# Retention attention and a top-2 mixture of experts on one core: a PSUM bank for VectorE's scratch, y in two parts, x's low part behind the routing steps

## The chip, the cores and the metric

The kernel runs on one core of a Trainium2 chip. A core has five engines that work side by side: PE (TensorE, matmuls into PSUM), DVE (VectorE), ACT (ScalarE), POOL (GpSimd) and SP (it issues DMAs). The metric is the device time of one execution in microseconds (us); less is better.

## What is computed

The reference has two parts. A retention attention runs over 4 batches of 768 tokens with 8 heads of 64; its output x, 3072 tokens of 512 numbers, goes to a mixture of 8 experts, of which each token takes the two with the highest noisy logits.

```
gamma = 1.0 - 2.0 ** (-5.0 - np.arange(H))
for t in range(S):
    state = gamma * state + einsum('bhd,bhe->bhde', k[:, :, t], v[:, :, t])
    y[:, :, t] = scale * einsum('bhd,bhde->bhe', q[:, :, t], state)
...
noisy_logits = x @ w_gate + log1p(exp(x @ w_noise)) * noise
top2 = argpartition(-noisy_logits, 2, axis=1)[:, :2]
top2_w = softmax of the two logits
for e in range(E):
    for k in range(2):
        mask = top2[:, k] == e
        h = np.maximum(x[mask] @ w1[e], 0.0)
        out[mask] += top2_w[mask, k, None] * (h @ w2[e])
```

## The kernel before, in words

The order of the work on each engine is the order in which the code issues it; nothing moves an instruction afterwards.

**The chunk loop (L704 to L732)** runs over 24 chunks of 128 tokens, j = 0 to 23, six for each batch (c = j % 6). An iteration j holds pieces of several chunks. On PE stand in this order: `qk(j+1)` (L335, scores into PSUM tiles pA), `x_total(j-1)` (L371, one matmul that sums the squares of y(j-1) into a few columns called XSS), what the table `between` holds for j, `y_mm(j)` (L349: masked scores times v; L352: q times the state U, not in a batch's first chunk; L362: the state update into the tile pU, not in a batch's last chunk), `x_rows(j-2)` (L386), `logits(j-2)` (L399, L402, into the tile pL) and what the table `todo` holds for j. y goes to one of two PSUM tiles pY, so y(j) may be written only when all readers of y(j-2) are done.

From y two f16 numbers are made whose sum is x: `x_hi` (ACT, L376) and `x_lo` (DVE, L380), both after a power-of-two scale that DVE computes from XSS (L169, L170). DVE also masks the scores (`masked(j+1)`, L342). ACT copies the state from pU to U (L368), squares y (L357) and copies x's rows (L388).

**Routing** of a batch starts when its logits are there and is cut in steps that stand in `between` and `todo`, so that they run in the iterations of the next batch: route_a and route_b (noisy logits, the top 2, L412 to L438), route_b2 and route_c (one-hot masks, L445 to L469), route_d (places in the sorted lists, L491 to L511, it reads pL), route_e (two parts, L521 and L525, it prepares a table), table (PE, L532), route_f (DVE, L537 or L539, it copies the table's result out of pL) and route_w (gates, L477 to L484). In the last iterations of a batch's turn, route_d stands at j = 10, 16 and 22 behind `x_lo(j-1)`. DVE's scratch for these steps lies in PSUM, in the columns of pU behind the state, so in the tile that PE writes at L362 and ACT reads at L368.

**The weights** of the first two experts come in f32 and are cut in f16 high and low parts during the loop: w_sum and w_hi and part of w_scaled on ACT (L193, L214, L226), w_scaled and w_rest on POOL (L228, L232), their scale on PE and DVE (L196, L203).

**After the loop** `early(n)` issues n units of the first expert's matmuls (first its first matrix, L751 to L753, whose result ACT reads at L754 and DVE at L755; then its second, L790 to L792) between the routing steps of the last batch. `ranks()` (L552 to L577) orders the other seven experts by their number of tokens; it is cut in two halves with one unit behind each, then come route_w and three units more. The expert loop (L891 to L963) follows.

Of the kernel before, what the change touches and what calls it, by code (L numbers as in the profile page):

```python
# [10 lines left out]
F32 = mybir.dt.float32  # L11
# [83 lines left out]
def moe_kernel(ctx, tc, qT, kT, kt, vt, noise, wgn, w1, w2, ctab, qtab, xbuf, gbuf, out):  # L95
# [49 lines left out]
    PL = pL[:, 0:NC * 4 * E].rearrange("p (c s e) -> p c s e", c=NC, s=2)  # L145
    XSS = pR[:, 0:4]
    POS = pL[:, 200:200 + (NC + 1) * NL].rearrange("p (c e) -> p c e", c=NC + 1)
    LST = pL[:, 280:280 + NCOL]
    SUM = pL[:, 340:348]
    pU = psum.tile([128, 512], F32, name="pU")  # L150
    PU = pU[:, :HP * D].rearrange("p (a d) -> p a d", a=HP)

    def spare(o, n):
        return pU[:, HP * D + o:HP * D + o + n]

    lanes = spare(0, 64).bitcast(F16)
    blks = spare(64, NCOL // 2).bitcast(F16)
    lidx = spare(92, NL), spare(102, NL)
    cump = spare(112, NL)
    small = spare(124, 48)  # L160
    invp = [spare(172 + i * NC, NC) for i in range(2)]
    wide = spare(184, NC * NL).rearrange("p (c e) -> p c e", c=NC)

# [179 lines left out]

    def y_mm(j):
        c = j % NC
        pY = psum.tile([128, HP, C], F32, name="pY", bufs=2)
        for i in range(HP):
            for s in range(2):
                nc.tensor.matmul(pY[s * 64:s * 64 + 64, i, :], VP[j][:, 2 * i + s, :], AM[j][:, s, i, :],  # L349
                                 start=(i == 0), stop=True, skip_group_check=True)  # L350
        for i in range(HP if c else 0):
            nc.tensor.matmul(pY[:, i, :], U[c % 2][:, i, :], QS[j][:, i, :],  # L352
                             start=False, stop=True, skip_group_check=True)
        PY[j] = pY.rearrange("p a c -> p (a c)")
        SS[j] = work.tile([128, 1], BF, name="xss")
        with nc.allow_low_precision(reason="only the exponent of the sum is used"):
            nc.scalar.activation(junk[:, :DM], PY[j], AF.Square, accum_out=SS[j])  # L357
        if c < NC - 1:

            for i in range(HP):  # L360
                for s in range(2):
                    nc.tensor.matmul(PU[s * 64:s * 64 + 64, i, :], IN["kt", j][:, i * 128 + s * 64:i * 128 + s * 64 + 64],  # L362
                                     VP[j][:, 2 * i + s, :],
                                     start=(c == 0 and i == 0), stop=True, skip_group_check=True)
            un = U[(c + 1) % 2]
            for s in range(2):
                r = slice(s * 64, s * 64 + 64)
                nc.scalar.activation(un[r, :, r], PU[r], AF.Copy)  # L368

# [182 lines left out]
    def ranks():  # L552
# [15 lines left out]
        nc.vector.tensor_copy(eid, rk)  # L568
        yield
        tp = hp.tile(s4, F32, name="tp")  # L570
# [82 lines left out]

    between = {}
    for b in range(B - 1):
        n = (b + 1) * NC - 1
        steps = [(2, route_a, b), (3, route_b, b), (4, route_b2, b), (4, route_c, b), (5, route_d, b),
                 (6, route_e, b, 0), (7, route_e, b, 1), (8, table, b), (8, route_w, b)]
        if b == B - 2:
            steps = steps[:-3]  # L660
        else:
            between.setdefault(n + 9, []).append((route_f, b))
        between.setdefault(n + 5, []).append((places, b))
        if b == B0 - 1:

            between[n + 9] += [(rows_of, acc, 0, 3)]
            between.setdefault(n + 10, []).extend((gather, 0, t, 0, 128, B0 * S) for t in range(3))
            for t in range(3):
                at(n + 11, x_t, 0, t)
        for s in steps:  # L670
            at(n + s[0], *s[1:])
    at(0, gate_sum)
    at(1, gate_weights)
    for i in range(4):
# [5 lines left out]
        at(8 + i, w_load, 0, "2", i)  # L680
        at(12 + i, w_sum, 0, "2", i)
        at(17 + i, w_hi, 0, "2", i)
        at(18 + i, w_scaled, nc.scalar, 0, "2", i)
        between.setdefault((19, 20, 22, 23)[i], []).append((w_rest, 0, "2", i))
    for i in range(7):
# [7 lines left out]
    between.setdefault(10, []).append((w_scale, 0, "1"))  # L693
    between.setdefault(17, []).append((w_scale, 0, "2"))
    mid = SECOND // 128
# [8 lines left out]
    for j in range(NCH):  # L704
# [5 lines left out]
        if j + AHEAD < NCH:  # L710
            load(j + AHEAD, "qk")
        if j:
            x_total(j - 1)
            x_hi(j - 1)
        if j + 1 < NCH:
            masked(j + 1)
        if j:
            x_lo(j - 1)
        if j + AHEAD < NCH:
            load(j + AHEAD, ("v", "kt"))  # L720
        if j >= 3:
            x_store(j - 3)
        for f, *a in between.get(j, []):
            f(*a)
# [3 lines left out]
        if j >= 2:  # L728
            x_rows(j - 2)
            logits(j - 2)  # L730
        for f, a in todo.get(j, []):
            f(*a)  # L732
    x_store(NCH - 3)
# [104 lines left out]
    x_lo(NCH - 1)  # L838
    route_e(b - 1, 1)
    early(1)  # L840
    x_rows(NCH - 1)
# [7 lines left out]
    for t in range(3, mid + 1):  # L849
        x_t(0, t)  # L850
    early(1)
    route_a(b)
# [23 lines left out]
    early(1)  # L876
    for piece in ranks():
        early(1)
    route_w(b)
    early(3)  # L880
    out_scale(0, 3, mid)
# [185 lines left out]
```

## Time and profile before

| | us |
|---|---|
| median of 3 runs | 684.81 (684.1 to 686.17) |
| the profiled execution's own time | 685.8 |
| its span, from the first to the last instruction | 684.0 |
| PE busy within the span | 651.6 (95%) |
| ACT busy | 318.7 (47%) |
| POOL busy | 291.5 (43%) |
| DVE busy | 278.1 (41%) |
| mean granted clock of TensorE | 0.981 |

A line of the timeline has the start of a group of like instructions in us from the start of the span, the time from its first start to its last end, the engine, the line of the kernel, the operation with output and input, the number of instructions, and in brackets how long the engine stood idle ahead of it and what ended that. Matmuls overlap, so the time that a group takes from PE is best read from start to start. The granted clock is 1.00 when TensorE runs at 2.4 GHz and 0.50 at 1.2 GHz. In the expert loop PE is at work almost without a break; its idle time lies in the chunk loop, in the routing behind it and at the two ends.

### The profile page before, as it was taken

Reading aid. Unit: us, or ns where it says so; the run is one execution under the profiler, and the core shown is the slowest. Engines: PE = TensorE matmul, PEld = TensorE weight load, DVE = VectorE, ACT = ScalarE, POOL = GpSimd, SP = SyncE. Lnnn points to the kernel's source line nnn. Section 1 sums busy time; section 2 is a strip of 40 time slices with the busy share of each in tenths; the row PEclk is TensorE's granted clock in tenths of the full one; section 3 lists DMA queues with packets and bytes.
Section 4 is the critical chain, followed back from the end, with each engine's and each line's share of the span. In section 5 each row is a group of like instructions: output and inputs, shape, how many; then the busy total and the mean of one; then the engine's idle time right before and its main releaser. Section 6 shows DMA issues by size and latency. Waiting matters only on the chain. (4 is left out here: it accounts for less than half of the span.)

```text
span 684.0 us, 12921 instructions
## 1 busy us (share of the span) xinstructions
PE 651.6 (95%) x5165; PEld 395.5 (58%) x5165; DVE 278.1 (41%) x765; ACT 318.7 (47%) x564; POOL 291.5 (43%) x226
## 2 busy tenths in 40 slices
PE   8999898998999999999999999999999999999991
PEld 5888787655666545654555455545554565456440
DVE  4768696774135435342144214420532152225100
ACT  5698777621157425452544345433543454434110
POOL 4547797312432534533443345234524451443131
PEclk9999899999999999999999999999999999999996
DMA  9999896424798435753665467446644663661132
GB/s 342 357 406 406 305 394 233 127 65 86 283 165 201 149 68 126 181 187 60 127 162 191 74 110 200 156 77 120 182 157 92 124 172 140 111 125 14 17 46 33
DMA packets 95230, 112.36 MB, mean 164 GB/s; under 512 B 62208, under 2 KB 62464, under 8 KB 91584
## 3 DMA queue, kind: packets, MB, share of 16 engines
q1 hardware_dynamic: 81472, 84.03, 37.5%
q0 software_dynamic: 13120, 26.63, 21.6%
q8 instruction: 42, 0.69, 0.4%
q10 hardware_dynamic: 576, 0.84, 0.4%
q14 instruction: 20, 0.16, 0.1%
HBM read 72.03 MB, written 26.34 MB: 144 GB/s over the span
## 5 line engine op out<-in xcount | busy, mean ns | idle before, releaser
L781 POOL DMA_INDIRECT out<-ot,idx x54 | 88.0, 1630 | 263.0 <-ACT ot L776 139.4
L751 PE MATMUL pH<-xe,w1h 128*128 128x384 f16 (+4 forms) x544 | 176.3, 324 | 2.8 <-DVE hl L755 2.7
L752 PE MATMUL pH<-xe,w1h 128*128 128x384 f16 (+4 forms) x544 | 176.3, 324 | 1.7 <-issue 1.7
L753 PE MATMUL pH<-xe,w1l 128*128 128x384 f16 (+4 forms) x544 | 176.3, 324 | 0.0
L755 DVE SCALAR_TENSOR_TENSOR hl<-pH,hh 128x384 f16<-128x384 f32 (+4 forms) x136 | 74.4, 550 | 214.1 <-ACT hh L754 195.5
L792 PE MATMUL pO<-w2h,hl 128*128 128x512 f16 x384 | 145.5, 379 | 0.0
L791 PE MATMUL pO<-w2l,hh 128*128 128x512 f16 x384 | 145.5, 379 | 0.0
L790 PE MATMUL pO<-w2h,hh 128*128 128x512 f16 x384 | 145.5, 379 | 0.0
L754 ACT ACTIVATE hh<-pH 128x384 f16<-128x384 f32 (+4 forms) x136 | 65.6, 484 | 130.6 <-PE pH L753 120.8
L776 ACT ACTIVATE ot<-pO,gse 128x512 f32<-128x512 f32 (+4 forms) x54 | 37.1, 686 | 174.1 <-PE pO L792 163.5
L645 POOL DMA_INDIRECT gx<-gbuf,idx x54 | 68.2, 1264 | 37.2 <-DMA gbuf<-gateb 21.5
L219 DVE SCALAR_TENSOR_TENSOR w1l<-wst,wsc,w1h 128x1024 f16<-128x1024 f32 x28 | 35.7, 1284 | 99.0 <-ACT w1h L214 96.3
L752 PEld LDWEIGHTS <-w1h 128*128 128x128 f16 x544 | 53.5, 98 | 37.1 <-issue 4.3
L753 PEld LDWEIGHTS <-w1l 128*128 128x128 f16 x544 | 53.5, 98 | 35.1 <-issue 1.1
L751 PEld LDWEIGHTS <-w1h 128*128 128x128 f16 x544 | 54.1, 99 | 32.9 <-issue 0.2
L635 POOL DMA_INDIRECT xg<-xbuf,idx x55 | 53.7, 976 | 42.3 <-issue 15.5
L193 ACT ACTIVATE junk<-wst 128x1024 bf16<-128x1024 f32 x64 | 67.0, 1047 | 0.1
L792 PEld LDWEIGHTS <-hl 128*128 128x128 f16 x384 | 37.5, 98 | 45.4
L790 PEld LDWEIGHTS <-hh 128*128 128x128 f16 x384 | 38.1, 99 | 44.1
L791 PEld LDWEIGHTS <-hh 128*128 128x128 f16 x384 | 37.5, 98 | 44.0
L308 POOL TENSOR_TENSOR vp<-in_v,ct 128x512 f32<-128x512 f32 x24 | 25.1, 1044 | 33.3 <-issue 21.3
L214 ACT ACTIVATE w2h<-wst,wsc 128x1024 f16<-128x1024 f32 x32 | 36.5, 1139 | 0.0
(173 smaller groups left out, 750.6 us busy)
## 6 DMA issues: line engine op xcount, KB each, us to landing
wst<-w SPq DMA_DIRECT2D x28, 1024.0 KB
in_q<-qT SPq DMA_DIRECT2D x24, 256.0 KB
in_k<-kT SPq DMA_DIRECT2D x24, 256.0 KB
in_v<-vt SPq DMA_DIRECT2D x24, 256.0 KB
xbuf<-xr SPq DMA_DIRECT2D x24, 256.0 KB
out<-zero SPq DMA_DIRECT2D x6, 1024.0 KB
in_kt<-kt SPq DMA_DIRECT2D x20, 256.0 KB
wst<-w SPq DMA_DIRECT2D x8, 512.0 KB
```

The lines of the kernel that those rows point to most:

```text
L193: nc.scalar.activation(junk, st[:, i * 1024:(i + 1) * 1024], AF.Square, accum_out=ss[:, i:i + 1])
L635: nc.gpsimd.indirect_dma_start(out=x[:p1], out_offset=None, in_=xbuf[:128 + rows], in_offset=bass.IndirectOffsetOnAxis(ap=idx[:p1, i:i + 1 ...
L645: nc.gpsimd.indirect_dma_start(out=GX[e][:, t, :], out_offset=None, in_=gbuf[:128 + rows], in_offset=bass.IndirectOffsetOnAxis(ap=idx[:, i ...
L751: nc.tensor.matmul(p[:, :n], whi, xh, start=(k == 0), stop=False)
L752: nc.tensor.matmul(p[:, :n], whi, xl, start=False, stop=False)
L753: nc.tensor.matmul(p[:, :n], wlo, xh, start=False, stop=(k == KT - 1))
L754: nc.scalar.activation(hh[:, f, n0:n1], p[:, :n], AF.Relu)
L755: nc.vector.scalar_tensor_tensor(hl[:, f, n0:n1], p[:, :n], 0.0, hh[:, f, n0:n1], op0=OP.max, op1=OP.subtract)
L781: nc.gpsimd.indirect_dma_start(out=out, out_offset=bass.IndirectOffsetOnAxis(ap=idx[:n, i:i + 1], axis=0), in_=ot[:n], in_offset=None, com ...
L790: nc.tensor.matmul(p, a, WT["2h"][:, f, :], start=(f == 0), stop=False)
L791: nc.tensor.matmul(p, a, WT["2l"][:, f, :], start=False, stop=False)
L792: nc.tensor.matmul(p, c, WT["2h"][:, f, :], start=False, stop=(f == FT - 1))
```

## The change

1. **PSUM.** DVE's scratch moves from pU to pR, which is then used by nothing else. XSS moves from pR to pL, the tile of the logits and places. pU holds the state alone.
2. **y in two parts.** `y_in(j)` (the masked scores times v) is cut out of `y_mm(j)` and stands ahead of `x_total(j-1)`; `masked(j+1)` stands ahead of `x_hi(j-1)`. U's part stays behind `between`.
3. **x's low part.** `x_lo(j-1)` moves to the end of iteration j, behind everything that `between` and `todo` issue there. route_a moves behind it (table `late`).
4. **Weights.** For the first expert's second matrix w_sum comes two iterations later, w_hi too, its scale at 19 instead of 17; of w_scaled on ACT one piece stays in the loop and three move behind it, together with all four w_rest on POOL.
5. **ranks()** is issued in one piece, then route_w, then four units in a row.

```
-    XSS = pR[:, 0:4]
+    XSS = pL[:, 352:356]
-    lanes = spare(0, 64).bitcast(F16)
...
+    lanes = pR[:, 0:64].bitcast(F16)
...
-        steps = [(2, route_a, b), (3, route_b, b), (4, route_b2, b), (4, route_c, b), (5, route_d, b),
+        late.setdefault(n + 2, []).append((route_a, (b,)))
+        steps = [(3, route_b, b), (4, route_b2, b), (4, route_c, b), (5, route_d, b),
```
```
-        if j:
-            x_total(j - 1)
-            x_hi(j - 1)
         if j + 1 < NCH:
             masked(j + 1)
-        if j:
-            x_lo(j - 1)
...
+        y_in(j)
+        if j:
+            x_total(j - 1)
+            x_hi(j - 1)
         for f, *a in between.get(j, []):
             f(*a)
...
         for f, a in todo.get(j, []):
+            f(*a)
+        if j:
+            x_lo(j - 1)
+        for f, a in late.get(j, []):
             f(*a)
```
```
-        at(12 + i, w_sum, 0, "2", i)
-        at(17 + i, w_hi, 0, "2", i)
-        at(18 + i, w_scaled, nc.scalar, 0, "2", i)
-        between.setdefault((19, 20, 22, 23)[i], []).append((w_rest, 0, "2", i))
+        at(14 + i, w_sum, 0, "2", i)
+        at(19 + i, w_hi, 0, "2", i)
+    at(23, w_scaled, nc.scalar, 0, "2", 0)
...
     route_e(b - 1, 1)
+    for i in range(1, 4):
+        w_scaled(nc.scalar, 0, "2", i)
+        w_rest(0, "2", i - 1)
...
-    for piece in ranks():
-        early(1)
+    ranks()
     route_w(b)
-    early(3)
+    early(4)
```

Three places show it in the engines' own order. On PE, in an iteration without a state update, before (pA are the scores, pR holds XSS, pY is y):

```order
L335 MATMUL pA<-qs,in_k 128x128 x8
L371 LDWEIGHTS oneb
L371 MATMUL pR<-xss,oneb 128x1
L349 MATMUL pY<-am,vp 64x128 x8
L352 MATMUL pY<-qs,U_162 128x128 x4
```

and after:

```order
L331 MATMUL pA<-qs,in_k 128x128 x8
L344 MATMUL pY<-am,vp 64x128 x8
L369 LDWEIGHTS oneb
L369 MATMUL pL<-xss,oneb 128x1
L350 MATMUL pY<-qs,U_162 128x128 x4
```

y's first part has moved ahead of the sum of squares of the chunk before. On DVE in iteration 10, before, from the masking of the scores of chunk 11 to the start of route_d (L491); x_1011 is the x of chunk 9:

```order
L342 TENSOR_TENSOR am<-pA,ct 128x512 x2
L380 SCALAR_TENSOR_TENSOR x_1011<-pY,upx,x_1011 128x512
L203 TENSOR_REDUCE s_1029<-pL 128x1
L169 TENSOR_SCALAR p2m<-s_1029 128x1
L170 TENSOR_SCALAR wsc_489<-p2m 128x1
L173 TENSOR_SCALAR wsc_489<-p2m 128x1
L491 TENSOR_TENSOR pU<-pL,cb 128x60
L492 TENSOR_TENSOR sl<-pL,cb 128x60
```

and after, from route_d's first instruction (L489) to the masking for chunk 12; x_1027 is the x of chunk 9:

```order
L489 TENSOR_TENSOR pR<-pL,cb 128x60
L490 TENSOR_TENSOR sl<-pL,cb 128x60
L492 TENSOR_TENSOR ps<-pL,cb 128x60
L493 SCALAR_TENSOR_TENSOR pR<-pR,sl 128x60
L494 TENSOR_TENSOR pR<-pL,cb 128x10
L500 TENSOR_TENSOR t<-pR,oh 128x120
L504 TENSOR_REDUCE pR<-t 128x12
L505 CAST pR<-pR 128x12
L506 TENSOR_SCALAR pR<-pR 128x12
L507 TENSOR_SCALAR pR<-pR 128x12
L509 CAST lf<-pR 128x24
L378 SCALAR_TENSOR_TENSOR x_1027<-pY,upx,x_1027 128x512
```

x_lo (L380, now L378) has moved from ahead of route_d to behind its last instruction. On DVE at ranks(), before (hl is the low part of a unit's result):

```order
L567 TENSOR_REDUCE rk<-cm 128x7
L568 CAST eid<-rk 128x7
L755 SCALAR_TENSOR_TENSOR hl<-pH,hh 128x192
L572 TENSOR_TENSOR tp<-acc,pm 128x343
L573 TENSOR_REDUCE tk<-tp 128x49
L547 TENSOR_SCALAR padv<-tk,ct 128x49
```

and after, at the same place:

```order
L565 TENSOR_REDUCE rk<-cm 128x7
L566 CAST eid<-rk 128x7
L569 TENSOR_TENSOR tp<-acc,pm 128x343
L570 TENSOR_REDUCE tk<-tp 128x49
L545 TENSOR_SCALAR padv<-tk,ct 128x49
```

The unit's instruction has left the middle of ranks(); the four of its kind now stand in a row behind route_w's last instruction (L482).

## Rows read from the trace of the kernel before

**Rows 1.** The page: busy time, share of the span and instructions of each engine.

```profile
PE 651.6 (95%) x5165; PEld 395.5 (58%) x5165; DVE 278.1 (41%) x765; ACT 318.7 (47%) x564; POOL 291.5 (43%) x226
```

**Rows 2.** The timeline of PE in iteration 8, from one qk to the next, at full clock.

```profile
42.96 1.16 PE L335 MATMUL pA<-qs,in_k 64*128 64x128 f32 x16
...
44.16 1.09 PE L349 MATMUL pY<-am,vp 128*64 128x128 f32 x16
45.19 1.16 PE L352 MATMUL pY<-qs,U 128*128 128x128 f32 x8
46.27 0.69 PE L362 MATMUL pU<-vp,in_kt 128*64 128x64 f32 x16
46.89 0.62 PE L386 MATMUL pX<-id,x 128*128 128x128 f16 x8
...
47.63 0.38 PE L335 MATMUL pA<-qs,in_k 64*128 64x128 f32 x2
```

**Rows 3.** The timeline of PE from iteration 10 to the last y: the qk of iterations 10, 14, 15, 20 and 21, the stalls between, and y(23).

```profile
52.30 1.16 PE L335 MATMUL pA<-qs,in_k 64*128 64x128 f32 x16
...
77.55 0.18 PE L399 MATMUL pL<-wg,x 128*128 128x32 f16 x1 [2.35 <-DVE acc L537]
...
77.84 2.08 PE L335 MATMUL pA<-qs,in_k 64*128 64x128 f32 x16
...
85.36 0.38 PE L335 MATMUL pA<-qs,in_k 64*128 64x128 f32 x2
...
95.15 0.18 PE L399 MATMUL pL<-wg,x 128*128 128x32 f16 x1 [0.88 <-DVE s L203]
...
111.10 0.18 PE L399 MATMUL pL<-wg,x 128*128 128x32 f16 x1 [2.35 <-DVE acc L539]
...
111.37 1.99 PE L335 MATMUL pA<-qs,in_k 64*128 64x128 f32 x16
...
117.93 1.16 PE L335 MATMUL pA<-qs,in_k 64*128 64x128 f32 x16
...
120.04 0.19 PE L458 MATMUL pL<-mb,trib 128*128 128x60 bf16 x1 [0.84 <-DVE mb L448]
...
124.02 1.09 PE L349 MATMUL pY<-am,vp 128*64 128x128 f32 x16
```

**Rows 4.** Windows: the stretch, its length, busy time of PE, PEld, DVE, ACT and POOL with the number of instructions, granted clock, DMA share, GB/s.

```profile
78.00:84.00 6.00, 6.00 (x43) 5.21 (x45) 3.81 (x26) 2.59 (x4) 3.36 (x2) 0.50 1.04 396
94.00:97.00 3.00, 2.12 (x36) 1.84 (x35) 2.93 (x12) 2.66 (x4) 3.00 (x4) 1.00 1.05 398
112.00:114.00 2.00, 2.00 (x21) 1.76 (x19) 1.93 (x11) 2.00 (x3) 1.50 (x2) 0.50 0.38 136
170.00:172.00 2.00, 2.00 (x14) 1.84 (x13) 0.89 (x6) 0.00 (x0) 0.00 (x0) 0.50 0.26 24
```

**Rows 5.** The timelines of PE and of DVE at the end of iteration 10: the last logits, the next qk and x_total; route_d from its first instruction, the scale of the chunk behind it, and a x_lo. Then DVE's x_lo in iteration 14.

```profile
57.27 0.17 PE L402 MATMUL pL<-wg,x 128*128 128x16 f16 x1
57.37 1.16 PE L335 MATMUL pA<-qs,in_k 64*128 64x128 f32 x16
58.46 0.18 PE L371 MATMUL pR<-xss,oneb 128*128 128x1 bf16 x1
...
57.56 0.23 DVE L491 TENSOR_TENSOR pU<-pL,cb 128x60 f32<-128x60 f32 x1 [0.64 <-ACT U L368]
...
59.79 0.15 DVE L169 TENSOR_SCALAR p2m<-pR 128x1 int32<-128x1 int32 x1
...
61.24 0.74 DVE L380 SCALAR_TENSOR_TENSOR x<-pY,upx,x 128x512 f16<-128x512 f32 x1
...
76.62 0.75 DVE L380 SCALAR_TENSOR_TENSOR x<-pY,upx,x 128x512 f16<-128x512 f32 x1 [1.78 <-ACT x L376]
```

**Rows 6.** The timeline of DVE in iteration 11: route_e from its first instruction to the scale behind it.

```profile
61.90 0.50 DVE L521 TENSOR_TENSOR bb<-pU,lf 128x336 f16<-128x336 f16 x1
...
63.83 0.15 DVE L169 TENSOR_SCALAR p2m<-pR 128x1 int32<-128x1 int32 x1
...
64.08 1.28 DVE L342 TENSOR_TENSOR am<-pA,ct 128x512 f32<-128x512 f32 x2
```

**Rows 7.** The timelines of DVE and of PE at ranks(): the unit's instruction between its halves, the second half, route_w's first instruction, the next units; and PE's matmuls of these units, the first and the last of the 39 ahead of a stall, the stall, and the first start at full clock after 21 matmuls.

```profile
165.36 0.36 DVE L755 SCALAR_TENSOR_TENSOR hl<-pH,hh 128x192 f16<-128x192 f32 x1 [4.63 <-ACT hh L754]
165.64 0.76 DVE L572 TENSOR_TENSOR tp<-acc,pm 128x343 f32<-128x343 f32 x1
...
168.13 0.16 DVE L477 TENSOR_SCALAR pU<-den 128x6 f32<-128x6 f32 x1
...
169.49 0.88 DVE L755 SCALAR_TENSOR_TENSOR hl<-pH,hh 128x192 f16<-128x192 f32 x3
...
163.79 0.25 PE L751 MATMUL pH<-xe,w1h 128*128 128x192 f16 x1
...
166.93 0.25 PE L753 MATMUL pH<-xe,w1l 128*128 128x192 f16 x1
169.89 0.32 PE L751 MATMUL pH<-xe,w1h 128*128 128x192 f16 x1 [2.72 <-DVE hl L755]
...
173.08 0.25 PE L751 MATMUL pH<-xe,w1h 128*128 128x192 f16 x1
```

**Rows 8.** The timeline of PE: the longest stall behind that.

```profile
183.78 0.27 PE L752 MATMUL pH<-xe,w1h 128*128 128x256 f16 x1 [1.14 <-issue]
```

More of the change, by code (lines that the diff above doesn't have):

```diff
@@ L149, in moe_kernel @@
     SUM = pL[:, 340:348]
[L150 to L154, printed above, removed]
-    lanes = spare(0, 64).bitcast(F16)
[L157 to L162, printed above, removed]
+    XSS = pL[:, 352:356]
+    pU = psum.tile([128, HP, D], F32, name="pU")
+    lanes = pR[:, 0:64].bitcast(F16)
+    blks = pR[:, 64:64 + NCOL // 2].bitcast(F16)
+    lidx = pR[:, 92:92 + NL], pR[:, 102:102 + NL]
+    cump = pR[:, 112:112 + NL]
+    invp = [pR[:, 128 + i * 8:128 + i * 8 + NC] for i in range(2)]
+    wide = pR[:, 144:144 + NC * NL].rearrange("p (c e) -> p c e", c=NC)
+    small = pR[:, 208:208 + 48]
     def pow2(ss, target, up, down=None):
@@ L342, in masked, with y_in, y_mm @@
             nc.vector.tensor_tensor(AM[j][:, s], pA[s], mask[:, None, :].to_broadcast([128, HP, C]), op=OP.mult)
-    def y_mm(j):
-        c = j % NC
-        pY = psum.tile([128, HP, C], F32, name="pY", bufs=2)
+    def y_in(j):
+        PY[j] = psum.tile([128, HP, C], F32, name="pY", bufs=2)
         for i in range(HP):
             for s in range(2):
-                nc.tensor.matmul(pY[s * 64:s * 64 + 64, i, :], VP[j][:, 2 * i + s, :], AM[j][:, s, i, :],
+                nc.tensor.matmul(PY[j][s * 64:s * 64 + 64, i, :], VP[j][:, 2 * i + s, :], AM[j][:, s, i, :],
                                  start=(i == 0), stop=True, skip_group_check=True)
+    def y_mm(j):
+        c, pY = j % NC, PY[j]
         for i in range(HP if c else 0):
@@ L361, in y_mm @@
                 for s in range(2):
-                    nc.tensor.matmul(PU[s * 64:s * 64 + 64, i, :], IN["kt", j][:, i * 128 + s * 64:i * 128 + s * 64 + 64],
+                    nc.tensor.matmul(pU[s * 64:s * 64 + 64, i, :], IN["kt", j][:, i * 128 + s * 64:i * 128 + s * 64 + 64],
                                      VP[j][:, 2 * i + s, :],
@@ L367, in y_mm @@
                 r = slice(s * 64, s * 64 + 64)
-                nc.scalar.activation(un[r, :, r], PU[r], AF.Copy)
+                nc.scalar.activation(un[r, :, r], pU[r], AF.Copy)
     def x_total(j):
@@ L568, in ranks @@
         nc.vector.tensor_copy(eid, rk)
-        yield
         tp = hp.tile(s4, F32, name="tp")
@@ L651, in x_t @@
         nc.sync.dma_start_transpose(XE[e][:, :, o + p0:o + p1], x[p0:p1])
-    between = {}
+    between, late = {}, {}
     for b in range(B - 1):
         n = (b + 1) * NC - 1
-        steps = [(2, route_a, b), (3, route_b, b), (4, route_b2, b), (4, route_c, b), (5, route_d, b),
+        late.setdefault(n + 2, []).append((route_a, (b,)))
+        steps = [(3, route_b, b), (4, route_b2, b), (4, route_c, b), (5, route_d, b),
                  (6, route_e, b, 0), (7, route_e, b, 1), (8, table, b), (8, route_w, b)]
@@ L693, in moe_kernel @@
     between.setdefault(10, []).append((w_scale, 0, "1"))
-    between.setdefault(17, []).append((w_scale, 0, "2"))
+    between.setdefault(19, []).append((w_scale, 0, "2"))
     mid = SECOND // 128
@@ L850, in moe_kernel @@
         x_t(0, t)
+    w_rest(0, "2", 3)
     early(1)
```

## The prediction

> **What bounds the kernel now.** I read the page first: PE is busy for 651.6 of a span of 684.0 us [rows 1]. So what can be won lies in PE's idle time and in stretches of low clock, and I went through PE's timeline for both. In the expert loop there is next to nothing. The losses that the change touches lie between iteration 7 and the first expert's units. A full iteration takes PE 4.67 from qk to qk, 42.96 to 47.63 [rows 2]. Against that stand two stalls of 2.35, in iterations 14 and 20, where the logits' matmul (writes pL) waits until DVE has copied the table's result out of pL (L537, L539), and shorter ones of 0.88 and 0.84 [rows 3]. DVE is late there because x_lo stands ahead of the copy and waits 1.78 for x_hi on ACT [rows 5], where at that time the passes over the weights run. Behind both long stalls the granted clock is 0.50, 1.2 instead of 2.4 GHz [rows 4], and the iteration takes 77.84 to 85.36 = 7.52 in one case and 111.37 to 117.93 = 6.56 in the other [rows 3]: 2.85 and 1.89 over 4.67. A third such place is ranks(): 2.72 idle, and then 21 matmuls at low clock [rows 4, 7].
>
> **Parts that cost nothing by themselves.** Scratch in a bank of its own takes DVE's waits for ACT's copy of the state away, such as 0.64 ahead of route_d [rows 5]. DVE isn't the bound there, so by itself this is worth nothing; it starts some steps earlier. y in two parts issues the same matmuls; it gives PE 1.03 of work (L349, 44.16 to 45.19 [rows 2]) ahead of x_total. If that cover were gone, x_total would only come 1.03 earlier, as before. The weights' passes taken out of the loop run beside the first expert's units, for which PE has its work queued; what they relieve is counted in the next part.
>
> **The loop: what goes.** From qk(11) at 52.30 to y(23) at 124.02 PE took 71.72 for 13 iterations [rows 3]. At full clock and without waits: 13 x 4.67 = 60.71; less 2 x 0.62 for the two chunks without a state update (46.27 to 46.89) and 2 x 1.08 for the two without U's part (45.19 to 46.27) [rows 2]; and, as an estimate, plus 1.7 for the small matmuls of places, tables and sums of weights. That is 59.0. So 12.7 are lost before: 2.35 + 2.35 + 0.88 + 0.84 in the stalls named, 2.85 + 1.89 by the clock, and 1.5 in gaps too short to name. In the new order x_lo no longer stands ahead of L537 and L539 nor ahead of the weights' scale, and a weights' pass less stands ahead of x_hi, so I let all 12.7 go.
>
> **The loop: what comes.** x_lo(j-1) is now the last on DVE in iteration j, and y_in(j+1) needs it, since pY has two tiles. In iterations 10, 16 and 22 it is queued behind route_d, and route_d's first instruction reads pL, so it can't start before this iteration's last logits. In the trace of before it starts at 57.56, the last logits end at 57.27 + 0.17 = 57.44 [rows 5]; the wait named there is ACT's, but 0.12 behind the logits there is hardly room for another. From its start to the next instruction behind it route_d takes 59.79 - 57.56 = 2.23, and x_lo takes 0.74 [rows 5]. PE meanwhile has only qk(j+2), which starts at 57.37 and takes 58.46 - 57.37 = 1.09 [rows 5]. So y_in(11) waits (57.56 - 57.37) + 2.23 + 0.74 - 1.09 = 2.07. In iteration 16 route_d has one step more, 0.2 by its neighbours: 2.27. Behind iteration 22 there is no qk left: 2.27 + 1.09 = 3.36. What is queued behind the waiting matmul is all of PE's chunk.
>
> Behind these come small ones. From y_in's start DVE and ACT need x_total (1.03 later, 0.18 long), two scale steps (63.83 to 64.08 = 0.25), route_e (61.90 to 63.83 = 1.93), and x_lo 0.74 [rows 2, 5, 6]: with hand-overs 4.2. PE gets back to y_in after 4.67 - 0.62 = 4.05 in a chunk without state update and 4.67 - 1.08 = 3.59 in one without U [rows 2]. That gives 0.2 and 0.6, twice each, and I add 0.3 as an estimate for the longer routing step in iteration 21: 1.9. New waits in all: 2.07 + 2.27 + 3.36 + 1.9 = 9.6. Bounds: none of the small ones, 7.7; the small ones doubled, 11.5. I take 9.6, since its terms come from the same instructions.
>
> The clock is the open price. Idle of 2.35 and 2.72 was followed by 0.50, idle of 0.88 was not (94 to 97, 1.00) [rows 3, 4, 7]. 2.07 and 2.27 are nearer to 2.35, so I let the clock fall at all three. A fall costs from 1.45 (21 matmuls from 169.89 to 173.08, 3.19, where 38 spacings from 163.79 to 166.93 show 0.083 each, so 1.74 [rows 7]) to 2.85. I take 1.89, the nearest kind of work, at y_in(23). At y_in(11) and y_in(17) I take 1.89 less the 0.8 of small waits behind, which a slower PE no longer meets: 1.1 each. Sum 4.1; the ends are 0 and 8.6.
>
> The loop then gives 12.7 - 9.6 - 4.1 = -1.0, a small loss.
>
> **ranks().** Before, DVE stands at the unit's L755 for 4.63, from 160.73 to 165.36, between the halves; the second half (165.64 to 168.13) and route_w (168.13 to 169.49) come behind it, and so the next units' L755 only at 169.49 [rows 7]. PE, which needs their tiles freed, waits 2.72 and then runs 21 matmuls at low clock [rows 7]. In the new order the second half and route_w, 2.49 + 1.36 = 3.85, fill 160.73 to 164.6, ahead of the first L755 that can start at 165.36. The stall goes, 2.72, and its clock, 1.45: 4.17. What is late next: nothing before the 1.14 at 183.78 [rows 8], which I leave as it is.
>
> **Sum.** 685.8 (the profiled execution's own time; its span of 684.0 and 1.8 around it) + 1.0 - 4.17 = 682.6. The median of the runs, 684.8, is 1.0 below the profiled execution, so 681.6.
>
> **Rivals.** (1) The clock holds at the two shorter waits. For it: they are shorter than any idle time that was followed by a fall. Then 1.1 + 1.1 less: 679.4; if it holds at the third too, 677.5. (2) x_lo isn't held, because route_d doesn't in fact wait for the logits. Then 2.07 + 2.27 + 3.36 and 4.1 for the clock go: 669.8. Against it: route_d reads what lies in pL beside the logits, and the 0.12. (3) What ranks() gives is given back: PE comes 4.17 sooner to the stall at 183.78, and what that waits for needn't come sooner. Then between 681.6 and 685.8, say 684.5. For it: that stall's releaser isn't an engine of the core's. (4) Slower: the clock falls and stays low. Waits of 0.3 and 0.7 follow within two chunks of each of the waits at y_in(11) and y_in(17); if these keep the clock at 0.50, each place costs what iteration 15 cost, 2.85 without anything taken off, or twice that over two chunks: 681.6 + 2 x 1.75 = 685.1 to 681.6 + 2 x 4.6 = 690.8. It decides against the change from 1.1 + (684.8 - 681.6) / 2 = 2.7 at each place. Against it: 0.88 idle alone left the clock at 1.00 [rows 4], and on a slower PE these waits vanish.
>
> The Trainium skill, "TensorE: Matmul & The Clock Gate", section "A second HAM failure mode: psum-queue depth-cycling", speaks for the last one: it tells of a kernel in which frequent short idles between groups of matmuls made the clock go down and up again and again, with the loss paid between the groups. By it the loop would land at the upper end of that rival; the one short idle in the rows above does not agree, and no run yet shows several behind a long one.
>
> **Chances and range.** The forecast 0.45, with a range of its own of 679 to 684 from the small waits' bounds; (1) 0.20; (2) 0.05; (3) 0.15; (4) 0.15. This kernel's runs can tell about 0.3% from no change, 2.05 us: faster is below 682.8, slower above 686.9. Faster: 0.7 of the forecast's 0.45, (1), (2) and a fifth of (3), 0.60. Slower: half of (4) and a little of (3), 0.10. Same: 0.30. The range leaves out (2) and the upper half of (4): 676 to 687.
>
> **What would show it.** In the profile after: y_in(11), y_in(17) and y_in(23) idle for about 2.1, 2.3 and 3.4 with x_lo as releaser (step right), or gone (rival 2); the granted clock behind each, 0.50 or 1.00 (rivals 1 and 4); no stall at L399 from DVE's copies; no stall of 2.72 at ranks(), and the stall near 183.78 no longer than 1.14 (rival 3). The forecast is wrong if a wait on another engine stands at the chunks where I let 12.7 go, above all on ACT, where the passes over the weights still run, or if the weights' passes moved behind the loop make the first expert's second matrix late.

## The result and the profile after

| | us |
|---|---|
| changed kernel, median of 13 runs | 690.13 (686.14 to 694.08) |
| kernel before on the same chip, median of 13 runs | 685.71 (683.32 to 690.26) |
| ratio | 1.0059 (95% interval 1.0036 to 1.0083) |
| the profiled execution's own time | 690.48 |

The change makes the kernel slower by 0.6%. The forecast was 681.6 with a range of 676 to 687. The page of the changed kernel answers to [rows 1] (span; then busy time, share and instructions of each engine):

```profile
span 688.6 us, 12859 instructions
...
PE 651.0 (95%) x5165; PEld 394.3 (57%) x5165; DVE 272.5 (40%) x765; ACT 318.5 (46%) x564; POOL 292.5 (42%) x226
```

PE has the same matmuls and is busy 0.6 less, so what the span grew by, 4.6, is idle time of PE. PE's timeline, the counterpart of [rows 3, 7, 8]: the long stalls, the qk of iterations 12, 14, 15 and 18, and the first expert's first matmul.

```profile
20.40 1.09 PE L344 MATMUL pY<-am,vp 128*64 128x128 f32 x16 [2.06 <-DVE x L378]
...
62.76 1.64 PE L344 MATMUL pY<-am,vp 128*64 128x128 f32 x16 [1.97 <-DVE x L378]
...
67.12 1.05 PE L331 MATMUL pA<-qs,in_k 64*128 64x128 f32 x14
...
72.49 1.09 PE L344 MATMUL pY<-am,vp 128*64 128x128 f32 x16 [0.63 <-DVE x L378]
...
76.30 1.16 PE L331 MATMUL pA<-qs,in_k 64*128 64x128 f32 x16
...
80.88 0.38 PE L331 MATMUL pA<-qs,in_k 64*128 64x128 f32 x2
...
88.05 0.19 PE L456 MATMUL pL<-mb,trib 128*128 128x60 bf16 x1 [0.30 <-DVE p2m L165]
...
93.99 1.97 PE L344 MATMUL pY<-am,vp 128*64 128x128 f32 x16 [2.17 <-DVE x L378]
...
98.28 0.49 PE L331 MATMUL pA<-qs,in_k 64*128 64x128 f32 x4
...
128.35 1.98 PE L344 MATMUL pY<-am,vp 128*64 128x128 f32 x16 [4.62 <-DVE x L378]
...
132.46 0.32 PE L751 MATMUL pH<-xe,w1h 128*128 128x384 f16 x1
...
189.43 0.37 PE L751 MATMUL pH<-xe,w1h 128*128 128x256 f16 x1 [2.41 <-DVE hl L755]
```

The stalls of 2.35 on the table's copies are gone, and iteration 14 takes 76.30 to 80.88, 4.58 instead of 7.38 (70.46 to 77.84). The qk's at 77.84, 85.36, 111.37 and 117.93 in [rows 3], counted from qk(11) at 52.30, open iterations 15, 16, 21 and 22, not 14, 15, 20 and 21. In the place of those stalls x_lo (L378) holds y_in (L344): at y(2), y(11), y(17) and y(23). The last four of the windows below are the counterpart of [rows 4] (length; busy time of PE, PEld, DVE, ACT and POOL; granted clock, DMA share, GB/s):

```profile
20.00:23.00 3.00, 2.60 (x41) 2.31 (x41) 2.76 (x12) 0.98 (x3) 0.00 (x0) 1.00 1.07 377
63.00:66.00 3.00, 3.00 (x24) 2.67 (x21) 2.31 (x9) 0.69 (x1) 3.00 (x3) 0.53 1.06 409
70.00:74.00 4.00, 3.37 (x55) 2.98 (x54) 3.86 (x13) 3.84 (x7) 3.88 (x3) 1.00 1.02 363
94.00:97.00 3.00, 3.00 (x22) 2.67 (x23) 1.98 (x6) 0.50 (x1) 2.06 (x2) 0.50 1.05 381
128.00:131.00 3.00, 2.65 (x20) 2.35 (x21) 0.69 (x4) 0.14 (x1) 0.00 (x0) 0.50 0.17 66
189.00:192.00 3.00, 2.58 (x13) 1.78 (x13) 1.03 (x3) 1.49 (x4) 0.00 (x0) 0.58 1.00 313
548.00:551.00 3.00, 3.00 (x12) 1.47 (x11) 0.00 (x0) 0.41 (x1) 1.16 (x1) 0.50 0.33 100
```

The clock is at 1.2 GHz behind the waits of 1.97, 2.17, 4.62 and 2.41, and once, at 548, with no long stall ahead of it. It stays at 2.4 GHz behind the 2.06 at y(2) and around the 0.63 at 72.49.

**Where the time went**, as PE's start of the same work, after minus before. At the qk of iteration 10 it is 54.20 against 52.30, +1.9: the wait at y(2). At y(23) it is 128.35 against 124.02, +4.3: the loop between lost 2.4. At the first expert's first matmul it is 132.46 against 126.79, +5.7: low clock behind y(23). Behind ranks() it is 176.43 against 175.31, +1.1: 4.6 are won back, 4.3 of them at ranks() itself (ahead of it 171.48 against 166.02, +5.5). Behind the new stall at 189.43 it is about 3.4, so 2.3 of that were given back; the stretch at 548 costs some 2 more, and PE ends at 674.42 against 668.95, +5.5. The last transfers make up 0.9, and the span is 4.6 longer. The first expert's first matmul in the kernel before:

```profile
126.79 0.32 PE L751 MATMUL pH<-xe,w1h 128*128 128x384 f16 x1
```

DVE's timeline shows what x_lo stands behind: in iteration 1 (the gate weights' scaling, not a routing step), in iteration 10 (route_d, from its first instruction on), and route_d's first instruction in iteration 22.

```profile
19.33 0.35 DVE L290 SCALAR_TENSOR_TENSOR wg<-wgf,gs,wg 128x128 f16<-128x128 f32 x1 [1.45 <-ACT wg L289]
19.60 0.74 DVE L378 SCALAR_TENSOR_TENSOR x<-pY,upx,x 128x512 f16<-128x512 f32 x1
...
59.73 0.23 DVE L489 TENSOR_TENSOR pR<-pL,cb 128x60 f32<-128x60 f32 x1 [1.75 <-PE pL L400]
...
61.96 0.74 DVE L378 SCALAR_TENSOR_TENSOR x<-pY,upx,x 128x512 f16<-128x512 f32 x1
...
125.03 0.23 DVE L489 TENSOR_TENSOR pR<-pL,cb 128x60 f32<-128x60 f32 x1 [3.84 <-PE pL L400]
```

Chips differ by 1% on the same kernel (the kernel before has medians of 685.61 and 686.88 on two of the chips below, of 677.39 to 679.79 on three), so each kernel is compared with the kernel before on its own chip, by ratio.

### The profile page after: what moved, and what is told of

Its sections match the earlier page's. It is cut to its first block, busy times and chain, and to the rows that moved or that the text cites. A ratio compares the mean times of both kernels' runs of the same rounds, so it can differ in the third digit from the quotient of the medians.

```text
span 688.6 us, 12859 instructions
## 1 busy us (share of the span) xinstructions
PE 651.0 (95%) x5165; PEld 394.3 (57%) x5165; DVE 272.5 (40%) x765; ACT 318.5 (46%) x564; POOL 292.5 (42%) x226
## 5 line engine op out<-in xcount | busy, mean ns | idle before, releaser
L781 POOL DMA_INDIRECT out<-ot,idx x54 | 89.4, 1655 | 264.9 <-ACT ot L776 136.2
L344 PE MATMUL pY<-am,vp 128*64 128x128 f32 x384 | 28.6, 295 | 12.4 <-DVE x L378 12.4
```

Of the source, the lines that this page charges most:

```text
L781: nc.gpsimd.indirect_dma_start(out=out, out_offset=bass.IndirectOffsetOnAxis(ap=idx[:n, i:i + 1], axis=0), in_=ot[:n], in_offset=None, com ...
```

## The experiments

### x_lo ahead of the routing step again

The whole change, with x_lo back ahead of `todo`, though still behind `between`, in every iteration (a1), in iterations 2, 10, 16 and 22 (a2), and in 1, 10, 16 and 22 (a3):

```
# a1
+        if j:
+            x_lo(j - 1)
         for f, a in todo.get(j, []):
             f(*a)
-        if j:
-            x_lo(j - 1)
# a2: front = j in (2, 10, 16, 22); a3: front = j in (1, 10, 16, 22)
+        if front:
+            x_lo(j - 1)
         for f, a in todo.get(j, []):
             f(*a)
-        if j:
+        if j and not front:
             x_lo(j - 1)
```

> The changed kernel with one thing undone: x_lo(j-1) stands ahead of the steps of todo again (behind between), in every iteration. Theory (what made the change slower is x_lo queued behind the routing steps): y(3), y(11), y(17) and y(23) no longer wait 2.06, 1.97, 2.17 and 4.62 for x_lo, and the low clock behind three of them goes; 10.8 + 2 to 4 less than the changed kernel, so 676 to 679, a ratio to before of 0.985 to 0.99. Rival (the time is set behind the loop, by the transfers for the first expert's last part and the second expert, and PE only waits there instead): the stalls go, but the stall near 189 grows by as much, ratio 1.00 to 1.005.

Measured: 683.2 against 686.88, ratio 0.9945 (0.9923 to 0.9966): a gain, but less than expected. The first expert's first matmul starts at 128.04 instead of 132.46, still 1.3 behind the first trace of the kernel before. PE's waits for x are down to 1.3. But p2m, the first step of the scale, reads XSS in pL, and PE's next matmuls into pL wait for it: 7.3, against 1.7 in the changed kernel.

```profile
PE pL L397 <- DVE p2m L165: 3.3, 4, 1.5
...
PE pL L456 <- DVE p2m L165: 2.0, 3, 1.5
PE pL L192 <- DVE p2m L165: 2.0, 1, 2.0
```

So "all late" is bad, and "none late" is not the best either.

> The changed kernel with x_lo ahead of the steps of todo only in iterations 2, 10, 16 and 22, behind them elsewhere. Theory: as the kernel before this one, 676 to 679, perhaps 1 better or worse; if the small waits of 0.6 behind (iterations 13, 19) matter, it is up to 1.5 slower than that one. Rival (x_lo behind the routing costs everywhere, not at four places): this one is clearly slower than the kernel before it, by 3 or more.

Measured: 682.93 against 686.88, 0.9946 (0.9922 to 0.9969), again above the 0.985 to 0.99 expected. The wait at y(2) was still 2.1: the x_lo that it needs, x_lo(0), is issued in iteration 1, not in 2. PE's waits in a2 (engine, line, what is waited for: us in total, times, longest):

```profile
PE pY L344 <- DVE x L378: 6.2, 6, 2.1
```

> As the kernel with x_lo ahead of the routing steps in iterations 2, 10, 16 and 22, with 1 in the place of 2: y(2) waits in iteration 2 for the x_lo of iteration 1, which stands behind the scaling of the gate weights. Theory A (what PE gains in the loop is capped: it waits at L192 for the second expert's weights, which arrive at a time of their own): the wait of 2.1 at y(2) goes, PE reaches the first expert's units 2 sooner, and waits 2 longer near 185 to 200; the time stays at 682 to 684, ratio 0.994 to 0.996. Theory B (no such cap): 2 less, ratio 0.991.

Measured: 679.03 against 685.61, 0.9894 (0.9859 to 0.9929). The theory that something else caps the gain fell. With four of the 23 x_lo put back, PE's waits for x go from 12.4 in the changed kernel to 4.1, the longest from 4.6 to 1.3 (same view, the changed kernel, then a3):

```profile
PE pY L344 <- DVE x L378: 12.4, 7, 4.6
```

```profile
PE pY L344 <- DVE x L378: 4.1, 5, 1.3
```

The first expert starts at 121.47 instead of 132.46, 11.0 sooner, and the ratios are apart by 0.0165, 11.3 us: what was won at the loop's end is still there at the end. So the x_lo's of these four iterations turn the change from a gain into a loss. The two kernels ran on different chips, and the gain of a3 and a4 was measured on one chip only.

Then a4, a3 with the first of seven expert numbers read alone on SP, so that the second expert's weights are asked for ahead of six reads:

```
-    for r in range(E - 1):
-        order.append(nc.sync.value_load(eid[0:1, r:r + 1], ...))
+    order.append(nc.sync.value_load(eid[0:1, 0:1], ...))
     for w in "12":
...
+    for r in range(1, E - 1):
+        order.append(nc.sync.value_load(eid[0:1, r:r + 1], ...))
```

> As the kernel before it, and SP loads the second expert's number alone and issues the loads of its weights at once, ahead of the six other numbers, so 3 to 4 sooner. Theory A (the weights' arrival caps the gain): the wait at L192 goes, 2 to 4 less than the kernel before it, ratio 0.988 to 0.992. Theory B (the arrival isn't the cap): within 1 of the kernel before it.

Measured: 677.67 against 685.61, 0.9877 (0.9842 to 0.9912), the lowest ratio of all. It is not told apart from a3.

### Each part alone, on the kernel before

b1, part 5: `ranks()` in one piece, then `early(4)`. b2, part 1: the scratch in pR, XSS in pL. b3, part 4: the weights' passes. b4, part 3: x_lo behind `todo`, route_a behind it. b6, part 2: y in two parts. The edits are those hunks of the diff above; in b6, without part 3, x_lo stands right behind x_hi.

> The kernel before with the last part of the change alone: ranks() in one piece, then route_w, then four units. The prediction's step: the stall of 2.72 and its low clock go, 4.2 less, ratio 0.994. Theory now: the stall goes, but PE then waits at the place near 180 to 185, where ACT and PE stand still until the gathers of that stretch are done, and gets 1 to 4 of it back; ratio 0.994 to 0.999.

Measured: 683.3 against 686.88, 0.9944 (0.9921 to 0.9966): a gain. In b1's trace a stall of the same kind then stands later:

```profile
185.13 0.37 PE L750 MATMUL pH<-xe,w1h 128*128 128x256 f16 x1 [2.83 <-DVE hl L754]
```

So in this trace part of what ranks() gives is given back, as in the changed kernel at 189.43.

> The kernel before with the first part of the change alone (scratch in pR, XSS in pL, the state alone in pU). The prediction's step: worth nothing by itself, ratio 0.998 to 1.001. Theory now (XSS in the tile of the logits makes PE's matmuls into pL wait until DVE has read the sum of squares, L397 behind L165, 1 to 3 in the changed kernels): new waits for p2m of 1 to 4 against fewer waits of DVE for ACT's copy; ratio 0.998 to 1.006.

Measured: 683.84 against 685.61, 0.9964 (0.9935 to 0.9993): a small gain, not nothing. The longest of PE's waits that come from XSS being in pL:

```profile
PE pL L367 <- DVE ps L490: 2.8, 1, 2.8
...
PE pL L367 <- DVE lg L412: 1.7, 2, 0.9
PE pL L192 <- DVE p2m L165: 1.5, 1, 1.5
```

x_total (L367) now waits for DVE's readers of the logits and places in the same tile. These three are new and sum up to 6.0; the stalls on the tables' copies are down from 2.3 to 1.0 each, 2.7 less. In b2's trace the first expert starts at 128.85, 2.1 later than in the first trace of before, so this trace shows no gain in the loop; where the gain comes from isn't shown. No run has the scratch's bank without XSS in pL, so the price of the one and the worth of the other aren't told apart.

> The kernel before with the fourth part of the change alone (later sums, high parts and scale of the second matrix, three scaled parts and all w_rest behind the loop). The prediction's step: a pass less on ACT ahead of x_hi, so the waits of 1.78 ahead of x_lo shrink, and with them the stalls of 2.35 in iterations 14 and 20 and their low clock: up to 9 less, ratio 0.987 to 0.995. Rival: ACT still has a pass ahead of x_hi there, the stalls shrink by one pass's 1.04 at most or not at all: ratio 0.996 to 1.001.

Measured: 683.28 against 685.61, 0.9963 (0.994 to 0.9986). The two stalls of 2.35 are down to 0.8 and 0.6:

```profile
PE pL L399 <- DVE acc L537: 0.8, 1, 0.8
...
PE pL L399 <- DVE acc L539: 0.6, 1, 0.6
```

So the weights' passes on ACT, not x_lo's place alone, made most of these stalls, and taking them out of the loop is enough to be rid of most of them. PE's list in b4, the next run, has no wait for acc either, with the passes in the loop; but there PE waits 24.5 for y, so that run doesn't tell what x_lo's place alone is worth to these stalls.

> The kernel before with the third part of the change alone: x_lo behind the routing steps, route_a behind it. Theory: three waits of y for x_lo of 2 to 4.6 appear, as in the changed kernel, and one in iteration 3, while the two stalls of 2.35 in iterations 14 and 20 go with their low clock: between 1 less and 6 more, ratio 0.999 to 1.009. If x_lo behind the routing were not the cause, the two stalls go and nothing comes: 9 less, ratio 0.987.

Measured: 710.44 against 686.88, 1.0336 (1.0296 to 1.0375): 23.6 us slower, far beyond what either theory expected. PE's and DVE's waits:

```profile
PE pY L349 <- DVE x L380: 18.9, 12, 2.3
PE pY L349 <- DVE p2m L169: 5.6, 2, 4.4
...
DVE pU L477 <- ACT U L368: 7.5, 2, 3.8
DVE oh L445 <- ACT U L368: 7.3, 3, 2.7
```

24.5 of PE's waits fall on y. The routing steps wait up to 3.8 for ACT's copy of the state, since their scratch lies in the tile pU, and x_lo now waits behind them.

> The kernel before with the second part of the change alone: y_in(j) ahead of x_total(j-1), masked(j+1) ahead of x_hi(j-1), x_lo right behind x_hi. The prediction's step: worth nothing by itself, ratio 0.998 to 1.002. Theory now (y_in gives PE 1.03 of work while DVE masks, so that x_total, the scale and x_hi come later by as much, with the copies out of pL behind them): between 1 more and 3 less, ratio 0.996 to 1.0015.

Measured: 686.1 against 678.28, 1.012 (1.0089 to 1.015): 7.8 slower. Its waits:

```profile
PE pL L401 <- DVE s L203: 2.5, 2, 2.3
PE pL L401 <- DVE acc L539: 2.3, 1, 2.3
PE pL L401 <- DVE acc L541: 2.3, 1, 2.3
PE pY L348 <- DVE x L382: 2.3, 4, 1.1
PE pU L364 <- ACT pU L423: 2.2, 2, 1.1
...
PE pU L364 <- DVE a L527: 1.0, 2, 0.7
```

The stalls on the tables' copies are as before. Against the kernel before, 2.3 on x, 2.2 on ACT's step in pU, 1.0 - 0.2 on a and 2.5 - 0.9 on s are new, 6.9 of the 7.8.

### Two parts together

e4: parts 2 and 3. e5: parts 1 and 3.

> The kernel before with the second and the third part of the change, scratch in pU, weights and ranks() as before. Alone the second part gave a ratio of 1.012 and the third 1.034. If they add, 1.046. Theory (y_in ahead of x_total gives DVE the time that a late x_lo needs, and with x_lo late nothing stands ahead of the copies out of pL): clearly less than the sum, 1.01 to 1.025.

Measured: 704.78 against 677.39, 1.0375 (1.0329 to 1.0421). The theory that the split pays for the late x_lo fell. The waits:

```profile
PE pY L348 <- DVE x L382: 27.9, 16, 3.4
...
DVE oh L447 <- ACT U L370: 9.2, 3, 3.4
```

> The kernel before with the first and the third part of the change: scratch in a bank of its own, XSS in pL, x_lo behind the routing steps; y in one part, weights and ranks() as before. The third part alone gave 1.034, and with the second 1.0375, so the second doesn't help it. Theory (with scratch in pU the routing steps wait for ACT's copy of the state, so the x_lo behind them comes at the end of the chunk every time; the bank of its own takes that away): 1.00 to 1.015. Rival (the bank has no part in it): 1.03.

Measured: 687.63 against 679.79, 1.0094 (1.0061 to 1.0128). From 1.0336 with part 3 alone, the scratch's own bank takes 2.4% off:

```profile
PE pY L345 <- DVE p2m L165: 5.7, 4, 2.3
PE pY L345 <- DVE x L376: 4.7, 2, 2.9
```

y's waits are 10.4 instead of 24.5, and no wait of DVE for ACT's copy of U stands among its long ones. So what a late x_lo costs depends on what the routing steps wait for. The parts alone give -0.36, +1.20, +3.36, -0.37 and -0.56%, together +3.3; the whole gives +0.59.

### What held y(23), and the first expert's stalls

c2: the transposes x_t of the last batch one iteration later. c3: the gathers too. d1: b1 with the second expert's gathers spread over the units.

```
# c2, e2, e3
-                at(n + 11, x_t, 0, t)
+                at(n + 12, x_t, 0, t)
# c3, besides
-            between.setdefault(n + 10, []).extend((gather, 0, ...) ...)
+            between.setdefault(n + 11, []).extend((gather, 0, ...) ...)
# d1
-                    for g in range((2, 2, 0, 1, 0, 1, 0, 1)[n]):
+                    for g in range((0, 0, 1, 1, 1, 1, 1, 2)[n]):
```

> The changed kernel with the first expert's three transposes of iteration 22 issued in iteration 23 instead. In the changed kernel y(23) waits 4.62, 1.26 over the 3.36 of the prediction, because route_d starts 1.30 after the end of the last logits there instead of 0.03 to 0.12 elsewhere. Theory A (the transposes, which start at 121.2 there, hold the signal from PE): route_d starts within 0.2 of the logits and y(23) waits 3.3 to 3.5. Theory B (the transposes have no part in it): 4.4 to 4.8 as before.

Measured, in one execution: 682.78, where the kernel before has 678.28; the wait at y(23) is 3.36.

> As the kernel before it, with the three gathers ahead of these transposes moved from iteration 21 to 22 too. Theory A2 (POOL's indirect transfers, which run from 114.6 to 123.8 in the changed kernel, hold the signals from PE to ACT and DVE while they run): the delay follows them; the U copy and Square of iteration 21 no longer start 1 late, and route_d in iteration 22 is as late or later. Theory B (neither has a part): both are as in the changed kernel.

Measured, in one execution: 682.23; the wait at y(23) is 3.35. Both seemed to show that the transposes had held y(23) for the 1.26 between 3.36 and 4.62. The unchanged copy on another chip shows that they didn't:

> The changed kernel once more, beside the next one on the same chip. If the 4.62 at y(23) belongs to the program, it is 4.4 to 4.8 here too, ratio 1.003 to 1.008; if it belongs to the chip of the first run, it is 3.3 to 3.5 where the next kernel has the same.

Measured: 681.96 against 677.39, 1.0055 (1.0035 to 1.0075), the same loss as on the first chip. PE at y(23):

```profile
128.58 0.83 PE L344 MATMUL pY<-am,vp 128*64 128x128 f32 x5 [3.37 <-DVE x L378]
```

The waits at y(2), y(11) and y(17) are 2.06, 1.97 and 2.17, as in the first trace, but the clock isn't the same: it fell behind y(2) and held behind y(11). The windows behind these two, and one at the place of the first trace's stall at 189.43 (columns as above):

```profile
24.00:27.00 3.00, 3.00 (x47) 2.86 (x48) 0.56 (x1) 2.92 (x8) 1.80 (x2) 0.63 0.90 344
65.00:68.00 3.00, 2.95 (x43) 2.75 (x45) 2.87 (x10) 1.33 (x4) 3.00 (x2) 1.00 1.02 369
190.00:193.00 3.00, 3.00 (x28) 2.50 (x26) 0.85 (x2) 3.00 (x9) 0.00 (x0) 1.00 1.03 280
```

> The changed kernel with the first expert's three transposes in iteration 23 instead of 22, on the same chip as the one before. Theory A (the transposes hold PE's signal): y(23) waits 3.4 here and 4.6 in the kernel before it, which is 1 to 2 slower. Theory B (the chip): both have the same wait, and the times agree within 1.

Measured: 681.65 against 677.39, 1.0059 (1.0033 to 1.0084), with 3.4 at y(23): moving the transposes does nothing. The 1.26 belongs to the first trace.

> x_lo ahead of the routing steps in iterations 1, 10, 16 and 22, the second expert's number loaded alone ahead of its weights, and the three transposes in iteration 23. Theory: as without the last of these, ratio 0.985 to 0.990, since no x_lo stands behind route_d in iteration 22 any more.

Measured (a4 with the later transposes): 675.72 against 677.39, 0.9961 (0.994 to 0.9981), outside the range expected, and less of a gain than a4's, on another chip. With the loop shorter, the first expert stands and waits for its transposed rows, which a4 doesn't:

```profile
PE pH L754 <- DMA xe<-xg: 4.3, 1, 4.3
```

> The kernel before with ranks() in one piece, and the second expert's gathers spread over the first expert's last units, (0, 0, 1, 1, 1, 1, 1, 2) in the place of (2, 2, 0, 1, 0, 1, 0, 1), so that no seven indirect transfers stand in a row on POOL. With ranks() in one piece alone PE is 5.1 ahead of the kernel before at the 15th unit and 2.5 ahead from the 25th on, because ACT starts a unit 3.9 late while the row of indirect transfers runs. Theory A (the row of transfers is what holds ACT): the stall of 2.8 near 184 shrinks to under 1, the time is 1 to 2.5 under that kernel, ratio 0.991 to 0.993. Theory B (it isn't): the stall stays, or the later gathers make the second expert late; ratio 0.994 to 1.0.

Measured: 676.13 against 678.28, 0.9972 (0.9949 to 0.9995). The stall of b1 at 185.13 is not there, but one on the gathered rows is, further on:

```profile
202.57 0.34 PE L750 MATMUL pH<-xe,w1h 128*128 128x416 f16 x1 [2.21 <-DMA xe<-xg]
```

So with the gathers spread PE waits for the rows instead. Whether the spreading took the stall of 2.83 away isn't shown: c2 and c3, with ranks() in one piece too and the gathers as before, have no such stall on this chip either.

> The kernel before once more, for its trace on a chip of these last runs. If the chips differ in what they make of the stretch behind ranks(), where ACT started 3.9 late on the first chips, the stall of 1.14 near 184 is gone or grown here; on a chip with times near 678 it should be gone, with the loop's times as in the first trace within 1.

Measured, in one execution on the chip of e5: 678.86. The first expert starts at 125.80, 1.0 sooner than in the first trace of before; the stall at ranks() is there, that of [rows 8] is not:

```profile
168.17 0.24 PE L751 MATMUL pH<-xe,w1h 128*128 128x192 f16 x1 [1.97 <-DVE hl L755]
```

So the stalls near 184 to 190 are not a property of the program alone.

## Why the prediction was wrong

**The step that failed is the loop's sum.** The forecast let the loop lose 1.0; in the first trace it lost 5.7 (PE's start at the first expert, 132.46 against 126.79). That is 4.7 of the 7.9 between the 682.6 forecast for the profiled execution and the 690.48 measured. Of the 4.7, 1.9 are the wait at y(2), which the forecast has not; 1.3 are y(23), 4.62 instead of 3.36; 1.1 are short waits in pL that stood at nothing (0.30 at 56.80 and at 88.05 and 0.25 at 105.10, all three for the scale's read of XSS, which part 1 put there, and 0.29 at 121.05). Some 0.4 are not put down to anything.

**"The loop: what goes" was right in its places.** The stalls of 2.35 and their low clock went: iterations 14, 15, 20 and 21 took 28.82 in all before and 18.66 after, 10.2 less. b3 shows that part 4 alone takes most of the idle time; the prediction named x_lo's place first.

**"The loop: what comes" had the right mechanism and a list that was too short.** The waits at y(11), y(17) and y(23) were foreseen as 2.07, 2.27 and 3.36 and measured 1.97, 2.17 and 4.62 (3.37 on another chip), the small ones at y(13) and y(19) as 0.6, measured 0.63; the releaser is x_lo each time. Missing is the same thing in iteration 1: there `todo` holds the gate weights' scaling, which waits 1.45 for ACT, x_lo(0) stands behind it, and y(2) waits 2.06. The prediction looked for x_lo only behind route_d, and began its sum at iteration 10. a2 and a3 differ just in whether iteration 1 or 2 is put back: 0.9946 and 0.9894. They ran on different chips, but the wait of 2.1 is in a2 and not in a3.

**Within the same step, the clock's price came out near the forecast, in part by luck.** The forecast let it fall at all three places for 4.1 in all; in the first trace it fell at all three. From y_in to the next qk, or to the first expert's matmul, a chunk without a state update takes 2.77 at full clock (before, 124.02 to 126.79); y(11) takes 67.12 - 62.76 = 4.36, y(17) 98.28 - 93.99 = 4.29 and y(23) 132.46 - 128.35 = 4.11, so 1.6, 1.5 and 1.3 more, 4.4 in all. In the copy on another chip (e1) it held behind the same 1.97 at y(11), as rival (1) has it for this place, fell at y(17) and y(23), and fell at y(2) too. So rival (1) is not borne out as a rule, and neither is its opposite.

Rival (4)'s mechanism is not borne out: the clock doesn't stay low, the window 70 to 74 with the 0.63 wait in it is at 1.00. Its price was met once: in e1 the low clock behind y(17) lasts into the next chunk, and from y(17) to the qk of iteration 19 PE takes 104.19 - 95.00 = 9.19 instead of 6.34 (34.13 to 40.47 in the changed kernel), 2.85 more, with no wait between. The rule that spoke for it, the Trainium skill's "TensorE: Matmul & The Clock Gate", section "A second HAM failure mode: psum-queue depth-cycling", is not borne out by these small waits; the slower outcome came by other ways.

**"Parts that cost nothing by themselves" was wrong for two of three.** y in two parts costs 1.2% when put into the kernel before alone (b6). Part 1 alone gains 0.36% (b2), but XSS in pL, which the prediction doesn't price, makes PE wait there: 6.0 in b2, 7.3 in a1, and in the changed kernel 1.7 for p2m, 0.89 of it behind the loop. And the bank is what makes part 3 bearable (b4 against e5). In the prediction's words a DVE that "starts some steps earlier" was worth nothing; but with x_lo behind those steps, DVE is what PE waits for. The Trainium skill's "PSUM — Partial Sum Buffer", section "PSUM bank collisions raise a hardware error", tells that a scheduler adds a dependency between instructions of two engines, ACT and DVE too, on one bank and the same 32 partitions; the waits `DVE oh <- ACT U` of 7.3 in b4 are of that kind, and they leave DVE's list of long waits when the scratch leaves pU (e5). The kernel before has 6.2 of them too, but there x_lo stands ahead of them.

**"ranks()" was right.** 4.17 forecast; 4.3 measured there, and b1 alone gives 0.56%, 3.6 us of its median. On another chip it has less to give: the stall of before is 1.97 there (e6), with the clock at 1.00 behind it.

**"What is late next: nothing" was wrong in the first trace**: 2.41 of stall at 189.43 with low clock behind it instead of 1.14 at 183.78, rival (3), 2.3 in all. In the copy on another chip the stretch from 190 to 193 has full clock and PE fully busy, and its ratio is the same, 1.0055; so rival (3) isn't what makes the change slow.

**The sum put right**, in the first trace: the loop's 5.7 in the place of 1.0 make 4.7; 2.3 given back and some 2 at 548 were not in the sum; 0.4 more won back between the first expert's start and the end of ranks(), and 0.9 at the last transfers, come off. That is 7.7 of the 7.9. The terms differ from chip to chip, though the ratio doesn't: between the traces of e1 and e6, taken on two chips, the loop loses 7.1 (first expert at 132.87 against 125.80), 2.3 come back by the end of ranks(), and the 4.7 that are left stay until PE's last matmul. In both the loss is made in the loop, and the 11.3 us between the changed kernel and a3 show that the four late x_lo's decide the sign.

**Still open**: why in the first trace route_d in iteration 22 started 1.3 late (125.03, although the last logits end at 123.73); what held ACT ahead of the stall at 189.43; why parts 1 to 5 together are less than their sum beyond what e5 explains.

## What to carry to other kernels

An instruction that another engine needs soon should not be queued behind one that waits; before moving it to the end of an iteration, list everything that stands there in every iteration, the one-time work of the first ones too. Put it back just at the places where such a wait stands: four of 23 turned +0.6% on one chip into -1.1% on another. Scratch that shares a PSUM tile with another engine's data cost little here while nobody queued behind its user and 2.4% once somebody did, so the parts of such a change have to be judged together. Whatever moves into another tile in exchange, as XSS into pL, has a price of its own.

## What the runs showed of the hardware

- The granted clock fell to 1.2 GHz behind idle times of 1.97 and 2.17, and not behind 2.06 in the same execution. In the copy on another chip (e1) it was at 0.63 in the stretch from 24 to 27, behind the same wait at y(2), and at 1.00 from 65 to 68, behind the same 1.97 at y(11); it was at 1.00 behind the 1.97 at ranks() too (e6, 168 to 172). The length of an idle time alone doesn't tell.
- The clock was also low at 548 to 551, behind a run of 16-column matmuls with one idle of 0.48 that the profile puts down to no engine.
- The same program takes 1% longer on some chips. Between 190 and 650 us PE of the kernel before was busy 458.84 of 460 in the first trace and 460.00 on another chip; that is 1.2 of the 7.0 between the two spans. PE's starts in the two traces show where the lead grows: 1.0 is there at the first expert (126.79 against 125.80), 3.2 behind ranks() (173.33 against 170.14), 5.1 behind the stall near 184 that one trace has and the other not (185.06 against 179.92), and 7.3 at the last matmul (668.57 against 661.30). What in the chips makes the difference is not shown.
